# Windowed attention with a soft mixture of experts on one core: loads tied to TensorE's instruction blocks, fewer small matmuls, reordered products

## The chip, the cores and the metric

The kernel runs on one core of a Trainium2 chip. The metric is the device time of one execution in microseconds (us), the median of several runs. TensorE is called PE here, its weight loads PEld, VectorE DVE, ScalarE ACT, GpSimd POOL and SyncE SP. SP issues every transfer of this kernel.

## The reference

Everything is float32. B = 8, H = 8 heads, 512 local and 32 global positions, head dimension 64, and a window of 32 positions to either side.

```python
s_g  = scale * q_g @ concat(k_g, k_l).T           # global queries see all keys
out_g = softmax(s_g) @ concat(v_g, v_l)
s_l  = concat(scale * q_l @ k_g.T, where(|i-j| <= 32, scale * q_l @ k_l.T, -1e9))
out_l = softmax(s_l) @ concat(v_g, v_l)
x = concat(out_g, out_l) as (4352, 512)           # one row per position and batch
logits = x @ phi                                    # 32 slots, 4 per expert
d = softmax over the rows;  c = softmax over the slots
slot_input = d.T @ x                                # 32 x 512
slot_out[e] = relu(slot_input[e] @ w1[e]) @ w2[e]   # 8 experts, 512 -> 1024 -> 512
out = c @ slot_out
```

## The kernel before, in words

The attention works on 32 units, `k` = 0 to 31, each a pair of heads of one batch `b = k // 4` (`s = k % 4` is the unit's place in its batch). The loop over `k` (L428) issues, in the order in which it is written, for each engine:

- loads on SP (L431 to L442): the queries `q` of unit k+1, the keys `k` of unit k+4, the values `v` of one or two later units, once per batch the global queries `qg`, and one or two pairs of expert weight pages `w` (512 KB each; `plan`, L422). Tiles are reused, so a load also waits until the last reader of its buffer is done: `q` has 2 buffers, `k` 5, `v` 4, `qg` 1. SP takes its loads strictly in the order of the program.
- `scores(k)` (L157) on PE: 8 bf16 matmuls write the mask, 32 small matmuls add 32 queries by 128 keys each, into `s`, for which there is one buffer.
- `shift(k)` (L173) on DVE: the row maximum `mx` (L176), then `e = s - mx` in two halves (L179). `e` also has one buffer, and `values(k-1)` reads the previous unit's `e`, so the subtraction waits for that.
- `values(k-1)` (L191) on PE: 32 small matmuls, softmax weights by values (`v` and the two shifted copies `va`, `vb` that POOL makes in `make_v`, L137), one for each 32 queries of a head.
- at s = 0 `global_scores` (L216, 32 matmuls into `gs` and `gm`), then its maximum `gmx` on DVE and its subtraction `sg` on POOL, both halves (L247). At s = 1 `global_transpose`, at s = 2 `global_values` (`og`, L262).
- `normalise(k-1)` (L201) on DVE: two short operations and the product `xh` (L209).
- `transpose_exp(k)` (L182): 8 transposes `t` on PE, two exponentials on ACT.
- `turn_x(k-1)` (L285): 4 transposes `xt` of `xh` on PE, a copy on ACT.
- small work on the logits of the batch before.

A float32 matmul is two weight loads and two matmuls for PE, so four instructions; a transpose or a bf16 matmul is two. The profile's counts of matmuls are after this split.

After the loop come the last logits, the slots' inputs, and the experts: `first_product(0)` (L600, `ph`, experts 0 to 3 side by side), `hidden(0)` (L620, on DVE `hs`, on PE the transposes `ht`, on ACT a copy), `first_product(1)`, `hidden(1)`, then `second_product` (L660, `po`) and the combination of the outputs (`combine`, L681), whose stores go out on SP. The two halves h of the output columns follow each other, and stores of h = 0 run beside matmuls of h = 1.

Of the kernel before, what the change touches and what calls it, by code (L numbers as in the profile page):

```python
# [15 lines left out]
NS = E * SE  # L16
# [25 lines left out]

def window(c):

    w = min(max(c, 1), 14)
    return ((w - 1) % 3, (w - 1) // 3)
# [9 lines left out]
def kernel(  # L56
# [14 lines left out]
    ctx.enter_context(tc.manual_schedule())  # L71

# [30 lines left out]
    npage = [0]  # L103
    slots = [(keep, f"pg{i}") for i in range(NWA // 2)]

    def load_pages():

        pool, tag = slots[npage[0] // 2]
        t = pool.tile([P, 2, 1024], F32, tag=tag, name=f"w{npage[0]}", bufs=1)
        for i in range(2):  # L110
            k, e, a, f = pages[npage[0]]
            nc.sync.dma_start(t[:, i, :], w1[e, a] if k == 0 else w2[e, a, f])
            wt[k, e, a, f] = t[:, i, :]
            npage[0] += 1
# [4 lines left out]
    def load_k(k):  # L119
        ks[k] = kp.tile([P, KC], F32, tag="k", name=f"k{k}", bufs=5)  # L120
        nc.sync.dma_start(ks[k], kT[k])

    def load_q(k):
        qs[k] = kp.tile([P, SL], F32, tag="q", name=f"q{k}", bufs=2)
        nc.sync.dma_start(qs[k], qT[k])

    def load_qg(b):
        qgs[b] = kp.tile([P, P], F32, tag="qg", name=f"qg{b}", bufs=1)
        nc.sync.dma_start(qgs[b], qG[b])
# [27 lines left out]
    def scores(k):  # L157
        ps = psS.tile([P, 2, 4, P], F32, tag="s", name=f"s{k}")
        for i in range(4):
            for r in range(2):  # L160
                nc.tensor.matmul(ps[32 * i:32 * i + 32, r], idm[64 * r:64 * r + 64, :],  # L161
                                 mk[64 * r:64 * r + 64, i:i + 4, :], start=True, stop=False)
        for t in range(4):
            for i in range(4):
                c = 4 * t + i
                for r in range(2):
                    nc.tensor.matmul(ps[32 * i:32 * i + 32, r, t, :], qs[k][64 * r:64 * r + 64, 32 * c:32 * c + 32],  # L167
# [5 lines left out]
    def shift(k):  # L173
# [4 lines left out]
        for r in range(2):  # L178
            nc.vector.tensor_tensor(e[:, r], ps[:, r], bc(mx[:, r], P), ALU.subtract)  # L179
        es[k] = e  # L180

    def transpose_exp(k):  # L182
        for r in range(2):
            pt = psT.tile([P, 4, P], F32, tag="t", name=f"t{k}_{r}")
            for t in range(4):
                nc.tensor.transpose(pt[:, t, :], es[k][:, r, t, :], ident)  # L186
# [4 lines left out]
    def values(k):  # L191
        po[k] = psV.tile([P, 2, 512], F32, tag="v", name=f"o{k}")
        for r in range(2):
            for t in range(4):
                for i in range(4):
                    cls, m = window(4 * t + i)
                    nc.tensor.matmul(po[k][32 * i:32 * i + 32, r, VD * t:VD * t + VD],  # L197
                                     es[k][:, r, t, 32 * i:32 * i + 32], (vs, vas, vbs)[cls][k][:, m, r, :],
                                     start=True, stop=True)
# [16 lines left out]
    def global_scores(b):  # L216
        s = kp.tile([P, 2, 5, P], F32, tag="sg", name=f"sg{b}")
        small = [psT.tile([P, P], F32, tag="t", name=f"gs{b}_{r}") for r in range(2)]
        main = [psT.tile([P, 4, P], F32, tag="t", name=f"gm{b}_{r}") for r in range(2)]

        def mm(dst, j, r, keys):
            nc.tensor.matmul(dst, qgs[b][64 * r:64 * r + 64, 32 * j:32 * j + 32], keys, start=True, stop=True)  # L222

        heads = [(j, r, ks[4 * b + j][64 * r:64 * r + 64, :], slice(32 * j, 32 * j + 32)) for j in range(4) for r in range(2)]
        for j, r, k, o in heads:
            back = bass.AP(k.tensor, k.offset + 32 * 10, [list(k.ap[0]), [-32, 3], [1, 32]])
            mm(small[r][o, 0:96].rearrange("p (a s) -> p a s", s=32), j, r, back)
        for j, r, k, o in heads:
            mm(small[r][o, 96:128], j, r, k[:, 32 * KPOS[14]:32 * KPOS[14] + 32])
        for r in range(2):  # L230
            nc.scalar.copy(s[:, r, 4, :], small[r])
        for a, c0 in ((0, 0), (64, 32 * KPOS[2])):
            for j, r, k, o in heads:
                mm(main[r][o, :, a:a + 64], j, r, k[:, c0:c0 + 256].rearrange("p (m s) -> p m s", s=64))
        for r in range(2):
            nc.scalar.copy(s[:, r, 0:4, :], main[r])  # L236
# [7 lines left out]
    def global_shift(b):  # L244
        for r in range(2):
            s = sg[b][:, r]
            nc.gpsimd.tensor_scalar(s, s, gm[b][:, r:r + 1], None, ALU.subtract)  # L247

    def global_transpose(b):
        pts = psT.tile([P, 2, P], F32, tag="t", name=f"tgs{b}")  # L250
        for r in range(2):
            nc.tensor.transpose(pts[:, r, :], sg[b][:, r, 4, :], ident)
        nc.scalar.activation(sg[b][:, :, 4, :], pts, AF.Exp, scale=SCALE)
        for r in range(2):
            pt = psT.tile([P, 4, P], F32, tag="t", name=f"tg{b}_{r}")
            for m in range(4):
                nc.tensor.transpose(pt[:, m, :], sg[b][:, r, m, :], ident)  # L257
# [4 lines left out]
    def global_values(b):  # L262
        pog[b] = psT.tile([P, 2, VD], F32, tag="t", name=f"og{b}")
        for r in range(2):
            for m in range(5):
                rows = P if m in (0, 4) else 96
                for j in range(4):
                    nc.tensor.matmul(pog[b][32 * j:32 * j + 32, r, :], sg[b][0:rows, r, m, 32 * j:32 * j + 32],  # L268
                                     vs[4 * b + j][0:rows, m if m < 4 else 5, r, :], start=(m == 0), stop=(m == 4))

    def global_normalise(b):
        o = pog[b]
        rc = xp.tile([P, 2], F32, tag="rg", name=f"rg{b}")
        nc.vector.tensor_scalar_add(rc, o[:, :, D], GUARD)
        nc.vector.reciprocal(rc, rc)
        n = xp.tile([P, 2, D], F32, tag="ng", name=f"ng{b}")
        nc.vector.tensor_tensor(n, o[:, :, 0:D], bc(rc, D), ALU.mult)
        p0 = 32 * (b % 4)
        for j in range(4):
            nc.gpsimd.tensor_copy(xg[p0:p0 + 32, P * j:P * j + P].rearrange("p (r d) -> p r d", r=2), n[32 * j:32 * j + 32])  # L280
# [4 lines left out]
    def turn_x(k):  # L285
        pt = psT.tile([P, 4, P], F32, tag="t", name=f"xt{k}")
        for t in range(4):
            nc.tensor.transpose(pt[:, t, :], xhs[k // 2][:, t, P * (k % 2):P * (k % 2) + P], ident)  # L288
# [3 lines left out]
    def turn_xg(i):  # L292
        pt = psT.tile([P, 4, P], F32, tag="t", name=f"xtg{i}")
        for hc in range(4):
            nc.tensor.transpose(pt[:, hc, :], xg[:, P * hc:P * hc + P], ident)
# [3 lines left out]
    def logits_mm(pl, b, hcs):  # L299
        for hc in hcs:  # L300
            for t in range(4):
                nc.tensor.matmul(pl[32 * t:32 * t + 32, :], phisb[:, hc, :], xTs[4 * b + hc][:, t, :],  # L302
                                 start=(hc == 0), stop=(hc == 3))

    def logits_g_mm(pl, i):
        for hc in range(4):
            nc.tensor.matmul(pl[96:128, :], phisb[:, hc, :], xTs["g", i][:, hc, :], start=(hc == 0), stop=(hc == 3))
# [38 lines left out]
    def turn(name, R):  # L346
# [3 lines left out]
        for i in range(2):  # L350
            nc.tensor.transpose(pt[:, i, 0:n], lgs[name][R, i, :], ident[R, R])
# [6 lines left out]
    def slot_sums(b):  # L358
        pa[b] = psT.tile([P, DM], F32, tag="t", name=f"pa{b}")
        for g in range(2):  # L360
            for t in range(4):
                nc.tensor.matmul(pa[b][32 * t:32 * t + 32, 256 * g:256 * g + 256], turned[b][:, 1, 32 * t:32 * t + 32],
                                 xhs[2 * b + g][:, t, :], start=True, stop=True)

    def slot_sums_g(i, p, g):
        nc.tensor.matmul(p[G, 256 * g:256 * g + 256], turned["g", i][:, 1, :], xg[:, 256 * g:256 * g + 256], start=True, stop=True)
# [31 lines left out]
    def turn_combine(b, src, n):  # L398
        pt = psT.tile([P, P], F32, tag="t", name=f"tc{b}")
        nc.tensor.transpose(pt[0:n, :], src, ident)  # L400
# [8 lines left out]
    for _ in range(NWARM):  # L409
        nc.tensor.matmul(pw, wrm[:, 0:P], wrm, start=True, stop=True)  # L410
# [11 lines left out]
    def plan(k):  # L422

        if k < 2:
            return 0
        return 1 if k % 2 == 0 or k > NK - 5 else 0

    for k in range(NK):  # L428
        b, s = k // 4, k % 4
        gb = b if s == 0 else b  # L430
# [360 lines left out]
```

## Time and profile before

| | |
|---|---|
| median of 3 runs | 340.04 us (337.43 to 343.75) |
| the profiled execution | 344.16 us |
| its span, first to last instruction | 342.3 us |
| PE busy (matmuls) | 258.7 us, 76% |
| DVE, POOL, ACT busy | 169.2, 128.6, 105.2 us |
| mean granted clock of PE | 0.915 |

The span is cut by stage in the profile's windows: the units take from 6.3 us to 262 us, the experts and the output the rest. A releaser "issue" after an idle time means that the engine waited for nothing that the profile can show: no semaphore, no other instruction.

### The profile page before, as it was taken

Reading aid. Unit: us, or ns where it says so; the run is one execution under the profiler, and the core shown is the slowest. Engines: PE = TensorE matmul, PEld = TensorE weight load, DVE = VectorE, ACT = ScalarE, POOL = GpSimd, SP = SyncE. Lnnn points to the kernel's source line nnn. Section 1 sums busy time; section 2 is a strip of 40 time slices with the busy share of each in tenths; the row PEclk is TensorE's granted clock in tenths of the full one; section 3 lists DMA queues with packets and bytes.
Section 4 is the critical chain, followed back from the end, with each engine's and each line's share of the span. In section 5 each row is a group of like instructions: output and inputs, shape, how many; then the busy total and the mean of one; then the engine's idle time right before and its main releaser. Section 6 shows DMA issues by size and latency. Waiting matters only on the chain.

```text
span 342.3 us, 15487 instructions
## 1 busy us (share of the span) xinstructions
PE 258.7 (76%) x6984; PEld 188.4 (55%) x6984; DVE 169.2 (49%) x360; ACT 105.2 (31%) x245; POOL 128.6 (38%) x190
## 2 busy tenths in 40 slices
PE   5767788668759779689679767688688897999830
PEld 4556577457637656476467556565676422455620
DVE  1456465645655357567575635467367213115520
ACT  1332244234223333442235213243243202104410
POOL 0375365337434544455385337345543000000000
PEclk9899899969998899999999969999899679999955
DMA  7875695827473647564785629278705959967796
GB/s 252 314 256 146 229 280 187 261 94 265 151 249 129 215 121 251 181 217 142 233 276 188 220 66 312 98 233 269 279 4 192 402 192 405 407 251 264 257 311 214
DMA packets 33761, 77.13 MB, mean 225 GB/s; under 512 B 3232, under 2 KB 13088, under 8 KB 33696
## 3 DMA queue, kind: packets, MB, share of 16 engines
q1 hardware_dynamic: 33696, 76.14, 64.8%
q8 instruction: 55, 0.90, 1.1%
q14 instruction: 10, 0.08, 0.1%
HBM read 67.22 MB, written 8.91 MB: 222 GB/s over the span
## 4 chain that ended last, share of the span: by engine, by line
PE 64%; issue 16%; DVE 10%; DMA 2%; ACT 2%; POOL 1%; SPq 1%; DVEq 0%; ACTq 0%; POOLq 0%
PE o L197 9%; PE s L167 9%; PE t L186 6%; PE xt L288 5%; PE po L665 4%; PE ph L605 4%; PE gm L222 4%; DVE e L179 3%; PE pc L691 3%; PE s L161 3%; PE og L268 3%; PE pl L302 3%; PE tg L257 2%; DMA qg<-in_qG_dram 2%; DVE xh L209 2%
## 5 line engine op out<-in xcount | busy, mean ns | idle before, releaser
L176 DVE TENSOR_REDUCE mx<-s 128x8 f32<-128x1024 f32 x32 | 39.2, 1225 | 60.0 <-PE s L167 59.9
L179 DVE TENSOR_TENSOR e<-s,mx 128x512 f32<-128x512 f32 x64 | 41.2, 686 | 33.8 <-PE o L197 31.5
L141 POOL COPY va<-v 128x650 f32<-128x650 f32 x32 | 23.2, 726 | 91.0 <-issue 52.3
L197 PE MATMUL o<-va,e 128*32 128x65 f32 x768 | 40.3, 227 | 14.9 <-issue 14.9
L187 ACT ACTIVATE e<-t 128x512 f32<-128x512 f32 x64 | 36.2, 603 | 35.3 <-PE t L186 34.1
L197 PE MATMUL o<-vb,e 128*32 128x65 f32 x512 | 38.1, 227 | 8.5 <-issue 8.4
L197 PE MATMUL o<-v,e 128*32 128x65 f32 x768 | 39.7, 227 | 4.9 <-issue 4.9
L167 PE MATMUL s<-k,q 64*32 64x128 f32 x2048 | 39.1, 276 | 3.8 <-issue 3.5
L197 PEld LDWEIGHTS o<-va,e 128*32 128x32 f32 x768 | 32.6, 113 | 13.7 <-issue 13.6
L186 PE MATMUL t<-con,e 128*128 128x128 f32 x256 | 38.3, 289 | 2.1 <-DVE e L179 1.8
L197 PEld LDWEIGHTS o<-v,e 128*32 128x32 f32 x768 | 31.8, 112 | 13.2 <-issue 12.2
L247 POOL TENSOR_SCALAR sg<-sg,gmx 128x640 f32<-128x640 f32 x16 | 29.9, 1883 | 24.0 <-DVE gmx L241 24.0
L167 PEld LDWEIGHTS s<-k,q 64*32 64x32 f32 x2048 | 33.4, 107 | 7.2 <-issue 5.3
L186 PEld LDWEIGHTS t<-con,e 128*128 128x128 f32 x256 | 30.5, 149 | 9.4 <-DVE e L179 5.7
L197 PEld LDWEIGHTS o<-vb,e 128*32 128x32 f32 x512 | 30.1, 112 | 10.1 <-issue 10.1
L288 PE MATMUL xt<-con,xh 128*128 128x128 f32 x128 | 20.3, 279 | 4.8 <-DVE xh L209 3.9
L142 POOL COPY va<-v 32x650 f32<-32x650 f32 x32 | 23.0, 719 | 2.0
L209 DVE TENSOR_TENSOR xh<-o,r 128x512 f32<-128x512 f32 x32 | 22.1, 692 | 1.6
L143 POOL COPY vb<-v 64x520 f32<-64x520 f32 x32 | 19.8, 618 | 1.9
L290 ACT COPY xT<-xt 128x512 f32<-128x512 f32 x32 | 18.9, 592 | 4.8 <-PE xt L288 4.7
L144 POOL COPY vb<-v 64x520 f32<-64x520 f32 x32 | 19.5, 611 | 1.8
L241 DVE TENSOR_REDUCE gmx<-sg 128x2 f32<-128x1280 f32 x8 | 11.9, 1486 | 14.2 <-ACT sg L236 14.2
(160 smaller groups left out, 385.2 us busy)
## 6 DMA issues: line engine op xcount, KB each, us to landing
w<-in_w_dram SPq DMA_DIRECT2D x64, 512.0 KB, 6.8
v<-in_vS_dram SPq DMA_DIRECT2D x32, 390.0 KB, 4.3
k<-in_kT_dram SPq DMA_DIRECT2D x32, 352.0 KB, 4.0
q<-in_qT_dram SPq DMA_DIRECT2D x32, 256.0 KB, 3.6
out_dram<-o SPq DMA_DIRECT2D x16, 512.0 KB, 5.4
qg<-in_qG_dram SPq DMA_DIRECT2D x8, 64.0 KB, 5.1
out_dram<-og SPq DMA_DIRECT2D x16, 32.0 KB, 2.9
con<-in_cst_dram SPq DMA_DIRECT2D x1, 362.0 KB, 4.6
```

What stands on the lines that cost most here:

```text
L141: nc.gpsimd.tensor_copy(va, v[:, 0:5])
L142: nc.gpsimd.tensor_copy(va[0:32], v[0:32, 1:6])
L143: nc.gpsimd.tensor_copy(vb[64:128], v[64:128, 0:4])
L167: nc.tensor.matmul(ps[32 * i:32 * i + 32, r, t, :], qs[k][64 * r:64 * r + 64, 32 * c:32 * c + 32], key_window(k, r, c), start=False, stop= ...
L176: nc.vector.reduce_max(mx, ps, axis=AX.X)
L179: nc.vector.tensor_tensor(e[:, r], ps[:, r], bc(mx[:, r], P), ALU.subtract)
L186: nc.tensor.transpose(pt[:, t, :], es[k][:, r, t, :], ident)
L187: nc.scalar.activation(es[k][:, r], pt, AF.Exp, scale=SCALE)
L197: nc.tensor.matmul(po[k][32 * i:32 * i + 32, r, VD * t:VD * t + VD], es[k][:, r, t, 32 * i:32 * i + 32], (vs, vas, vbs)[cls][k][:, m, r, : ...
L209: nc.vector.tensor_tensor(xhs[u][:, :, P * pp:P * pp + P].rearrange("p t (r d) -> p r t d", r=2), o[:, :, :, 0:D], bc(rc, D), ALU.mult)
L247: nc.gpsimd.tensor_scalar(s, s, gm[b][:, r:r + 1], None, ALU.subtract)
L288: nc.tensor.transpose(pt[:, t, :], xhs[k // 2][:, t, P * (k % 2):P * (k % 2) + P], ident)
```

## The change

1. **Loads in groups.** Every matmul and transpose that the program writes is counted (`counted`), 4 instructions for a float32 matmul and 2 otherwise, from an offset of 63. Where the count passes a multiple of 256, `begin_loads` takes loads from two waiting lists, up to 1,200 KB, and makes each wait for that very matmul. The first list holds `k`, `q`, `v` and `qg`, sorted by the unit that needs them; the second the weight pages, one at a time, which fill what room is left. `begin_due` starts a load without such a wait if no block came in time. `v` gets a fifth buffer, and `q` of unit k+2 is listed as soon as `scores(k)` stands in the program.
2. **Fewer matmuls.** In `values`, the two first and the two last 32-query blocks of a head share their window, so one matmul of 64 queries does both: 28 instead of 32. In `global_scores` one matmul of 512 columns (4 x 2 x 64) takes the place of two of 256: 24 instead of 32.
3. **Subtractions.** `e = s - mx` becomes one DVE instruction of 1,024 elements. Of the global subtraction, one half goes to DVE, the other stays on POOL.
4. **Order.** `turn_x(k-2)` stands between `scores(k)` and `values(k-1)`; before, `turn_x(k-1)` stood at the unit's end. Global work of batch 0 starts at unit 1, and the two halves of `global_values` go to units 2 and 3 of a batch (in the last batch both to unit 2).
5. **First products in a row.** `first_product(1)` follows `first_product(0)` directly; `hidden(0)` comes after it, and `hidden(1)` in the middle of the second product.

```diff
--- before.py
+++ after.py
@@ counting, and starting loads
+OFFSET = 63
+ROOM = 1200
...
+    pe = [OFFSET]
+    lines = [[], []]
+
+    def counted(i, n):
+        pe[0] += n
+        if pe[0] // 256 > (pe[0] - n) // 256:
+            begin_loads(i)
+        return i
+
+    def mm(out, lhsT, rhs, **flags):
+        return counted(nc.tensor.matmul(out, lhsT, rhs, **flags), 2 if lhsT.dtype == BF16 else 4)
+
+    def flip(out, x, idn):
+        return counted(nc.tensor.transpose(out, x, idn), 2)
+
+    def begin_loads(i):
+        room = ROOM
+        lines[0].sort(key=lambda load: load[1])
+        for line in lines:
+            while line and line[0][0] <= room:
+                size, due, load = line.pop(0)
+                room -= size
+                for d in load():
+                    tc.add_manual_dep(d.ins, i.ins.name, mybir.DependencyInfo(
+                        mybir.DependencyClass.Sync, mybir.DependencyReason.DATA))
+
+    def begin_due(k):
+        while any(due <= k for _, due, _ in lines[0]):
+            lines[0].pop(0)[2]()
...
     def load_v(k):
-        vs[k] = vp.tile([P, 6, 2, VD], F32, tag="v", name=f"v{k}", bufs=4)
-        nc.sync.dma_start(vs[k], vS[k])
+        vs[k] = vp.tile([P, 6, 2, VD], F32, tag="v", name=f"v{k}", bufs=5)
+        return [nc.sync.dma_start(vs[k], vS[k])]
@@ shift
-        for r in range(2):
-            nc.vector.tensor_tensor(e[:, r], ps[:, r], bc(mx[:, r], P), ALU.subtract)
+        nc.vector.tensor_tensor(e, ps, bc(mx, P), ALU.subtract)
@@ values
+        for t, i in ((0, 0), (3, 2)):
+            cls, m = window(4 * t + i)
+            for r in range(2):
+                mm(po[k][32 * i:32 * i + 64, r, VD * t:VD * t + VD], es[k][:, r, t, 32 * i:32 * i + 64],
+                   kinds[cls][k][:, m, r, :], start=True, stop=True)
         for r in range(2):
-            for t in range(4):
-                for i in range(4):
-                    cls, m = window(4 * t + i)
-                    nc.tensor.matmul(...)
+            for c in range(2, 14):
+                t, i = c // 4, c % 4
+                cls, m = window(c)
+                mm(...)
@@ global_scores
-        for a, c0 in ((0, 0), (64, 32 * KPOS[2])):
-            for j, r, k, o in heads:
-                mm(main[r][o, :, a:a + 64], j, r, k[:, c0:c0 + 256].rearrange("p (m s) -> p m s", s=64))
+        for j, r, k in heads:
+            four = bass.AP(k.tensor, k.offset, [list(k.ap[0]), [32 * KPOS[2], 2], [64, 4], [1, 64]])
+            product(main[r], j, r, four)
@@ global_shift
-        for r in range(2):
+        for r, eng in ((1, nc.vector), (0, nc.gpsimd)):
             s = sg[b][:, r]
-            nc.gpsimd.tensor_scalar(s, s, gm[b][:, r:r + 1], None, ALU.subtract)
+            eng.tensor_scalar(s, s, gm[b][:, r:r + 1], None, ALU.subtract)
@@ the first loads
+    load_k(1)
+    load_q(1)
     load_v(0)
-    load_k(1)
-    for k in (1, 2, 3):
-        if k > 1:
-            load_k(k)
+    load_k(2)
+    load_k(3)
     load_qg(0)
@@ the loop over k
-        if k + 1 < NK:
-            load_q(k + 1)
-        if k + 4 < NK:
-            load_k(k + 4)
-        for j in {0: (k + 1,), 1: (k + 1, k + 2), 2: (), 3: (k + 1,)}[s]:
-            if j < NK:
-                load_v(j)
-        if s == 1 and b + 1 < B:
-            load_qg(b + 1)
-        for _ in range(plan(k)):
-            if npage[0] < NWA:
-                load_pages()
+        part = global_parts(k)
+        begin_due(k)
         scores(k)
+        line_up("q", k + 2)
+        if k > 1:
+            turn_x(k - 2)
...
         shift(k)
         if k:
             values(k - 1)
-        if s == 0:
+        if "s" in part:
             global_scores(b)
...
-        if s == 2:
-            global_values(b)
+        for r in range(2):
+            if str(r) in part:
+                global_values(b, r)
...
-        if k:
-            turn_x(k - 1)
...
+        line_up_next(k)
+    lines[1].clear()
+    while npage[0] < NWA:
+        load_page()
@@ after the loop
     first_product(0)
+    first_product(1)
...
+    turn_combine(L, turned[L][:, 0, :], P)
+    turn_combine(B, cg.rearrange("p t s -> p (t s)"), 2 * NS)
     hidden(0, 0)
...
-    first_product(1)
-    turn_combine(L, turned[L][:, 0, :], P)
-    turn_combine(B, cg.rearrange("p t s -> p (t s)"), 2 * NS)
-    hidden(1, 0)
...
-    second_product(0, 0, 16)
+    second_product(0, 0, 8)
+    hidden(1, 0)
+    second_product(0, 8, 16)
     slot_outputs(0)
```

On SP, the loads around unit 7 of the kernel before. Names carry the unit (`q8` is the queries of unit 8, `w6` the pair of pages 6 and 7); the words in brackets are the engines and transfers that an instruction waits for.

```order
L125 DMA q8_1158<-in_qT_dram 128x512 [waits DMAHW6_49,PE_49]
L121 DMA k11_1160<-in_kT_dram 128x704 [waits DMAHW7_49]
L133 DMA v8_1162<-in_vS_dram 128x780 [waits DMAHW0_49,PE_49,Pool_49]
L125 DMA q9_1287<-in_qT_dram 128x512 [waits DMAHW2_49,DMAHW1_49,PE_49]
L121 DMA k12_1289<-in_kT_dram 128x704
L133 DMA v9_1291<-in_vS_dram 128x780 [waits DMAHW3_49,Pool_49]
L112 DMA w6_1293<-in_w1_dram 128x1024 [waits DMAHW4_49]
L112 DMA w6_1293<-in_w1_dram 128x1024 [waits DMAHW5_49]
```

The same place in the changed kernel: pages come singly, and each group starts with a load that waits for PE.

```order
L168 DMA q8_1011<-in_qT_dram 128x512 [waits DMAHW3_49,PE_49]
L164 DMA k10_1013<-in_kT_dram 128x704 [waits DMAHW4_49]
L153 DMA w2_893<-in_w1_dram 128x1024 [waits DMAHW5_49]
L164 DMA k11_1123<-in_kT_dram 128x704 [waits DMAHW6_49,PE_49]
L153 DMA w4_1125<-in_w1_dram 128x1024 [waits DMAHW7_49]
L168 DMA q9_1203<-in_qT_dram 128x512 [waits DMAHW0_49,PE_49]
L153 DMA w4_1125<-in_w1_dram 128x1024 [waits DMAHW1_49]
L176 DMA v9_1318<-in_vS_dram 128x780 [waits DMAHW2_49,PE_49,Pool_49]
```

These loads are the groups `q8 k10 w2`, `k11 w4`, `q9 w4` and the start of the one with `v9`; the first load of each waits for PE, and those behind it for no further place in PE's program.

On PE, the end of unit 7 and the start of unit 8 before: the transposes `t7`, then `xt6`, then the masks of `s8`.

```order
L186 MATMUL t7_0_1268<-con_78,e7_1207 128x128 x3
L186 MATMUL t7_1_1274<-con_78,e7_1207 128x128 [waits DVE_49,PE_49]
L186 MATMUL t7_1_1274<-con_78,e7_1207 128x128 x3
L288 MATMUL xt6_1280<-con_78,xh3_1252 128x128 [waits DVE_49,Activation_49]
L288 MATMUL xt6_1280<-con_78,xh3_1252 128x128 x3
L161 LDWEIGHTS con_78
L161 MATMUL s8_1296<-con_78 32x512 [waits PE_49]
L161 LDWEIGHTS con_78
```

The changed kernel, the end of `scores(8)` and the start of `values(7)`. Lines 88 and 91 are the helpers through which every matmul and transpose now goes.

```order
L88 LDWEIGHTS con_78
L88 MATMUL s8_1250<-con_78 32x512
L88 MATMUL s8_1250<-k8_810,q8_1011 32x128 [waits DMAHW6_49,DMAHW3_49]
L88 MATMUL s8_1250<-k8_810,q8_1011 32x128 x31
L91 MATMUL xt6_1291<-con_78,xh3_1213 128x128 [waits DVE_49,Activation_49]
L91 MATMUL xt6_1291<-con_78,xh3_1213 128x128 x3
L88 MATMUL o7_1302<-v7_806,e7_1149 64x65
L88 MATMUL o7_1302<-v7_806,e7_1149 64x65 [waits Activation_49]
```

`xt6` has moved from before `scores(8)` to behind it, and `values(7)` begins with matmuls of 64 queries.

On PE, the experts before: the end of the first product, then the transposes of the hidden layer, then the other first product.

```order
L605 MATMUL ph0_5277<-w12_2248,sT1_5232 32x512 x2
L605 MATMUL ph0_5277<-w14_2562,sT1_5232 32x512 x2
L630 MATMUL ht0_0_5334<-con_78,hs0_5331 128x128 [waits DVE_49]
L630 MATMUL ht0_0_5334<-con_78,hs0_5331 128x128 x3
L630 MATMUL ht0_1_5341<-con_78,hs0_5331 128x128 [waits DVE_49]
L630 MATMUL ht0_1_5341<-con_78,hs0_5331 128x128 x3
L605 MATMUL ph1_5368<-w16_2911,sT0_5231 32x512 x2
L605 MATMUL ph1_5368<-w18_3226,sT0_5231 32x512 x2
```

In the changed kernel the two first products touch.

```order
L88 MATMUL ph0_5133<-w12_2382,sT1_5088 32x512 x2
L88 MATMUL ph0_5133<-w14_2829,sT1_5088 32x512 x2
L88 MATMUL ph1_5171<-w16_3035,sT0_5087 32x512 x2
L88 MATMUL ph1_5171<-w18_3458,sT0_5087 32x512 x2
L88 MATMUL ph1_5171<-w16_3035,sT0_5087 32x512 x2
```

And the second half's hidden transposes stand inside the second product.

```order
L88 MATMUL po2_5272<-w36_4975,hT0_5227 32x256 x2
L88 MATMUL po2_5272<-w38_5040,hT0_5227 32x256 x2
L91 MATMUL ht1_0_5307<-con_78,hs1_5305 128x128 [waits DVE_49]
L91 MATMUL ht1_0_5307<-con_78,hs1_5305 128x128 x3
L91 MATMUL ht1_1_5314<-con_78,hs1_5305 128x128 [waits DVE_49]
L91 MATMUL ht1_1_5314<-con_78,hs1_5305 128x128 x3
L88 MATMUL po2_5272<-w40_5043,hT0_5227 32x256 [waits DMAHW2_49,Activation_49]
```

`ht0` and `ht1` are no longer directly behind the products whose results they turn.

## Rows read from the trace of the kernel before

**Rows 1.** Waits of PE, longest first: who waited for whom, us in total, times, longest.

```profile
PE o L197 <- issue: 28.2, 13, 4.6
PE og L268 <- issue: 7.1, 6, 1.6
PE xt L288 <- DVE xh L209: 3.9, 8, 0.5
PE s L167 <- issue: 3.5, 3, 1.7
PE tgs L252 <- POOL sg L247: 3.4, 3, 1.5
PE gs L222 <- DMA qg<-in_qG_dram: 3.2, 1, 3.2
```

**Rows 2.** Page, DMA queues: packets, MB, share of 16 engines.

```profile
q8 instruction: 55, 0.90, 1.1%
```

**Rows 3.** Timeline of PE, 25.9 to 31 us: start, us, line, xcount, idle before.

```profile
25.93 1.11 PE L268 MATMUL og<-v,sg 96*32 96x65 f32 x61 [0.83 <-issue]
26.97 1.09 PE L186 MATMUL t<-con,e 128*128 128x128 f32 x8
27.90 0.60 PE L288 MATMUL xt<-con,xh 128*128 128x128 f32 x4
28.43 0.41 PE L161 MATMUL s<-con 64*32 64x512 bf16 x8
28.66 0.90 PE L167 MATMUL s<-k,q 64*32 64x128 f32 x46
30.37 0.59 PE L167 MATMUL s<-k,q 64*32 64x128 f32 x18 [0.81 <-issue]
```

**Rows 4.** Chain of waits, pieces in order of time: start us, us, what.

```profile
66.50 4.56 issue
72.26 1.89 PE gm L222 x32
...
170.47 1.07 PE gm L222 x32
...
250.88 0.75 issue
```

**Rows 5.** Windows: us; PE, PEld, DVE, ACT, POOL busy; PEclk, DMA share, GB/s.

```profile
14.89:262.00 247.11, 190.15 (x6195) 151.43 (x6198) 142.75 (x298) 85.98 (x202) 125.13 (x180) 0.94 0.60 200
63.90:68.80 4.90, 2.60 (x130) 2.04 (x129) 1.97 (x5) 0.59 (x1) 0.40 (x1) 1.00 0.91 315
...
248.60:251.60 3.00, 2.28 (x146) 1.92 (x129) 1.90 (x3) 1.02 (x4) 0.83 (x2) 1.00 0.02 5
```

**Rows 6.** Chain of waits through one undisturbed unit, 130 to 136 us.

```profile
130.06 1.29 DVE e L179 x2
...
131.76 0.70 DVE xh L209
...
133.66 0.34 PE s L161 x8
...
134.95 1.05 PE o L197 x64
```

**Rows 7.** Page, costliest groups: busy us, mean ns, idle before, releaser.

```profile
L179 DVE TENSOR_TENSOR e<-s,mx 128x512 f32<-128x512 f32 x64 | 41.2, 686 | 33.8 <-PE o L197 31.5
...
L247 POOL TENSOR_SCALAR sg<-sg,gmx 128x640 f32<-128x640 f32 x16 | 29.9, 1883 | 24.0 <-DVE gmx L241 24.0
```

**Rows 8.** Timeline of PE, 281 to 296.5 us.

```profile
281.08 1.92 PE L605 MATMUL ph<-w,sT 128*32 128x512 f32 x16
285.54 1.32 PE L630 MATMUL ht<-con,hs 128*128 128x128 f32 x8 [2.53 <-DVE hs L627]
286.79 7.07 PE L605 MATMUL ph<-w,sT 128*32 128x512 f32 x64
...
296.04 0.64 PE L665 MATMUL po<-w,hT 128*32 128x256 f32 x8
```

More of the change, by code (lines that the diff above doesn't have):

```diff
@@ L103, with load_page @@
     npage = [0]
+    pair = [None]
     slots = [(keep, f"pg{i}") for i in range(NWA // 2)]
-    def load_pages():
[L108 to L114, printed above, removed]
+    def load_page():
+        n = npage[0]
+        pool, tag = slots[n // 2]
+        if n % 2 == 0:
+            pair[0] = pool.tile([P, 2, 1024], F32, tag=tag, name=f"w{n}", bufs=1)
+        k, e, a, f = pages[n]
+        wt[k, e, a, f] = pair[0][:, n % 2, :]
+        npage[0] += 1
+        return [nc.sync.dma_start(wt[k, e, a, f], w1[e, a] if k == 0 else w2[e, a, f])]
+    def load_pages():
+        for _ in range(2):
+            load_page()
     ks, qs, vs, qgs = {}, {}, {}, {}
@@ L306, in logits_g_mm @@
         for hc in range(4):
-            nc.tensor.matmul(pl[96:128, :], phisb[:, hc, :], xTs["g", i][:, hc, :], start=(hc == 0), stop=(hc == 3))
+            mm(pl[96:128, :], phisb[:, hc, :], xTs["g", i][:, hc, :], start=(hc == 0), stop=(hc == 3))
     G = slice(96, 128)
@@ L409 @@
     for _ in range(NWARM):
-        nc.tensor.matmul(pw, wrm[:, 0:P], wrm, start=True, stop=True)
+        mm(pw, wrm[:, 0:P], wrm, start=True, stop=True)
     load_k(0)
@@ L469 @@
         make_v(k)
-        if s == 0:
+        if "s" in part:
             global_max(b)
             global_shift(b)
-        if s == 2:
-            global_normalise(b)
+        for r in range(2):
+            if str(r) in part:
+                global_normalise(b, r)
         if k == 16:
@@ L488 @@
             combine_sum(("g", 0), cg[:, 0:1, :])
-        if s == 1:
+        if "t" in part:
             global_transpose(b)
@@ L572 @@
     mb = psT.tile([P, 1], F32, tag="t", name="mb")
-    nc.tensor.matmul(mb, mrow4.rearrange("p t s -> p (t s)"), con[0:1, C_ONE:C_ONE + 1], start=True, stop=True)
+    mm(mb, mrow4.rearrange("p t s -> p (t s)"), con[0:1, C_ONE:C_ONE + 1], start=True, stop=True)
     nc.vector.tensor_copy(rt, mb)
@@ L590 @@
         for hc in range(2):
[L591 removed]
+            mm(pst[:, hc, :], acc[:, 256 * i + P * hc:256 * i + P * hc + P], wm, start=True, stop=True)
         (nc.vector.tensor_copy if i else nc.scalar.copy)(sT[i], pst)
@@ L609, in first_product @@
                 tot = psT.tile([P, 1], F32, tag="t", name="tot")
-                nc.tensor.matmul(tot, qmat, wl, start=True, stop=True)
+                mm(tot, qmat, wl, start=True, stop=True)
                 nc.vector.tensor_scalar_add(rt, tot, GUARD)
@@ L673, in slot_outputs @@
         pq = psT.tile([P, 256], F32, tag="t", name=f"pq{h}")
-        nc.tensor.matmul(pq, qmat, so, start=True, stop=True)
+        mm(pq, qmat, so, start=True, stop=True)
         sas[h] = fin.tile([P, 256], F32, tag=f"sa{h}", name=f"sa{h}")
```

142 lines of the change are left out of this document (84 added, 58 removed).

## The prediction

> **What bounds the kernel now.** I read PE's waits first, then the DMA queues, then PE's timeline to see what the unexplained waits have in common, then the windows beside them, then the chain of waits.
>
> PE's longest waits have no releaser [rows 1]: 28.2 us in 13 waits in the values, 7.1 in 6 in the global values, 3.5 in 3 in the scores. Together that is 38.8 us in 22 waits; smaller groups I leave out. A queue of its own moved 0.90 MB in 55 packets, 16.4 KB each, marked as instructions [rows 2]. The timeline between two such waits, at 25.93 and 30.37 us, holds 61 + 8 + 4 + 8 + 46 = 127 matmuls, each with its weight load, so 254 instructions [rows 3], and 16.4 KB for some 256 instructions would be 64 bytes each. So PE seems to run out of program at the end of each block of 256, and the waits are those for the next block's transfer.
>
> How long PE waits hangs on the other transfers. The longest wait of all, 4.56 us [rows 4], follows a stretch in which the DMA engines were 0.91 busy; a wait of 0.75 us [rows 4] ends a stretch with a share of 0.02 [rows 5]. I take 0.75 us as what a dense block costs with free queues, and the rest as the time in which 16 KB stand behind megabytes.
>
> [...]
>
> **The change part by part.** All durations are of the profiled execution, 344.16 us (span 342.3 and 1.9 around it); that is 4.1 us over the median of the runs, 340.04.
>
> 1. Loads in groups. A group starts behind the matmul that opens a block, so the fetch of the next block, asked for at that time, should stand ahead of it. The 22 waits keep 0.75 us each, 16.5, and lose 38.8 - 16.5 = 22.3 us. Ends: nothing (the loads meet the fetches anyway) and all 38.8 (the rest hides in other waits). I take **-22.3**, since the quiet stretch shows that remainder directly.
>
> 2. Fewer matmuls. The 64 of one unit's values take 1.05 us [rows 6]; four products less are 8 of these 64, 0.13 us, and 32 units make 4.2 us. The global scores lose 8 of 32 products a batch, but their columns stay, so I give them nothing. Instructions fall by 8 x 2 x 32 for the values and 16 x 2 x 8 for the global scores, 768 or three blocks, at 0.75 each 2.3 us. **-6.5**; ends 0 (a wait for DVE fills the space) and -9.5 (three blocks at the present mean of 38.8/22 = 1.76 us, plus 4.2).
>
> 3. The move of the `xt` transposes and the single subtraction. In an undisturbed unit DVE's subtraction ends at 130.06 + 1.29 = 131.35 us, and PE begins the next unit's masks at 133.66 [rows 6], 2.31 us later, because `xt` first waits for `xh`, which ends at 132.46. In the new order the masks follow the 8 transposes, 27.90 - 26.97 = 0.93 us [rows 3]; with a hand-over about 1.0, so 1.3 us less. Against it: `xt` takes 28.43 - 27.90 = 0.53 us [rows 3] ahead of the values, for which the subtraction waits (31.5 us of DVE's idle time there [rows 7]); and the transposes lose their early start on the first half, half of 0.93. Net 1.3 - 0.53 - 0.47 = 0.3 us a unit, 31 units: **-9**. Ends: +6 (0.2 worse a unit, where the global work hides the gain) and -25 (0.8 better, where the values don't wait for `xt` but run under DVE's maximum).
>
> 4. The clock. [...] The global scores took 1.89 us directly after the longest wait and 1.07 us elsewhere [rows 4], so long waits are followed by slow work. [...]
>
> 5. The global subtraction. POOL loses 8 of its 16 instructions of 1.88 us [rows 7], and PE's 3.4 us of waiting for them [rows 1] can go. DVE gets 8 of 128x640; not in the trace, by its 686 ns for 512 elements [rows 7] 0.86 us each, 6.9 in all, delaying the next unit's maximum at most by that. DVE is busy 142.75 of 247.11 us there, so part is covered. **0**; ends -3.4 and +6.9.
>
> 6. The start. Batch 0's global scores move to unit 1, so the wait of 3.2 us for `qg` [rows 1] is gone: **-3.2**; ends -3.2 and 0, if `v0`, now behind three more loads, holds POOL instead.
>
> 7. The experts. Between the first products PE stands or transposes from 283.00 to 286.79 us, and from 293.86 to 296.04 before the second one [rows 8], 5.97 us together. Afterwards 1.3 us for each half's transposes and 0.4 for two others remain, 3.0: **-2.9**, the subtractions and copies running beside the products. The code from the second product to the stores is the same, so the end comes that much earlier; ends 0 and -3.4.
>
> 8. What grouping costs. The largest groups hold 1,170 KB, 1.20 MB. At 315 GB/s for a share of 0.91 [rows 5], 346 GB/s when full, that takes 3.5 us. The blocks of the units average (247 - 47) / 46 = 4.3 us, so a group usually ends in its block; where a dense block is over sooner, the next fetch still meets its tail. The wait is on SP: a load behind a group's first waits for PE too, and through it `scores` of a later unit. Queries are listed more than a unit ahead, and a group moves in 3.5 us, less than a unit. I take **+3**; ends 0 and +20, about 0.4 us in each block.
>
> Sum: -22.3 - 6.5 - 9 - 6 + 0 - 3.2 - 2.9 + 3 = -46.9, so 297.3 us in an execution like the profiled one, and 4.1 less for the median: **293 us**.
>
> **Rivals.**
>
> *The unit's chain takes it back.* When PE no longer waits for program, it waits for DVE: one buffer for the scores and one for `e` tie the units to maximum, values, subtraction, transposes. For it: the subtraction already waits 31.5 us for the values. Against it: DVE is busy 58% of the stage. Half of terms 1 and 4 and none of 2 and 3: -11 - 3 - 3.2 - 2.9 + 3 = -17, so 323 - 4 = about 319 us.
>
> *The rest hides too.* The blocks' last 0.75 us fall where PE waits for the subtraction anyway. Then term 1 is -38.8, 16.5 more: 277 us.
>
> *The count goes astray.* An instruction that waits twice may take a place in the program of its own; 101 of the changed kernel's PE instructions wait for two things, and the count leaves them out. At the end of the units groups would start some 90 instructions, a third of a block, late. If half of term 1's gain is lost for it, 11 us: 304 us.
>
> [...]
>
> *Loads come too late.* This one is slower. A load now starts only where PE has reached a place, and SP is in order, so one late group delays all behind it; if `q`, `k` or `v` land after they are wanted, PE stands, and reaches the next place later still. A whole group late is 3.5 us; half the units so, 16 x 3.5 = 56 us, gives 349 us. It decides from 47/3.5, some 13 units, on. Against it: only one transfer, the first `qg`, now holds PE for more than 3 us, and the mean DMA share of the stage is 0.60 [rows 5].
>
> **How the numbers follow.** The forecast has 0.48, the chain 0.17, the hidden rest 0.15, the count 0.10, other waits 0.05, late loads 0.05. The likeliest alone spans 284 to 304 us. With the chain and the rest's hiding within it the range is 276 to 319 us, which leaves about 0.15 outside. A measurement of this kernel tells about 2% from no change, so faster means under 333 us: nearly all cases but late loads, less the chance that several terms come out at their poor ends, 0.92. Within 2% is 0.04, slower 0.04.
>
> **What would show it.** Right: PE's waits without releaser fall from 38.8 us in these three groups to about 16, none much over 1.5 us; the granted clock of the units goes above 0.94; `xt` no longer waits for `xh`; the first products touch. Wrong: waits without releaser stay above 30 us (term 1); PE's waits for the subtraction or for POOL grow by more than 15 us (the chain); PE waits for `q`, `k` or `v` transfers (late loads); waits without releaser grow towards the end of the units (the count).

## The result and the profile after

The changed kernel takes 295.2 us, the median of four runs (292.14 to 300.01), beside 340.76 us for the kernel before: a ratio of 0.8661, 95% interval 0.8532 to 0.879. The forecast was 293 us. The profiled execution is the longest of the four, 300.01 us, at the lowest granted clock (0.947; the others 0.958 to 0.970), as that of before, 344.16, stood above its median; the two traces are compared with each other. A second trace of the changed kernel, of 296.22 us, belongs to the second measurement further on, and is named where it says something else.

The page of the changed kernel: span, busy time of each engine, the queue of the program's blocks, the engines' shares of the chain that ended last, and two groups of instructions (busy us, mean ns, idle before, releaser).

```profile
span 297.8 us, 14686 instructions
...
PE 255.7 (86%) x6600; PEld 181.9 (61%) x6600; DVE 174.5 (59%) x360; ACT 106.2 (36%) x245; POOL 121.6 (41%) x214
...
q8 instruction: 52, 0.85, 1.1%
...
PE 81%; issue 6%; DVE 4%; ACT 2%; DMA 1%; POOL 1%; SPq 0%; DVEq 0%; POOLq 0%; ACTq 0%
...
L221 DVE TENSOR_TENSOR e<-s,mx 128x1024 f32<-128x1024 f32 x32 | 39.2, 1224 | 25.2 <-PE o L88 21.5
...
L296 POOL TENSOR_SCALAR sg<-sg,gmx 128x640 f32<-128x640 f32 x8 | 17.3, 2164 | 12.0 <-DVE gmx L290 12.0
```

The span fell by 44.5 us and PE's busy time by 3.0 (from 258.7), so 41.5 us of the gain are time in which PE had stood. Three blocks fewer went through the queue of instructions [rows 2].

Waits of PE in the changed kernel: who waited for whom, us in total, times, longest.

```profile
PE o L88 <- issue: 5.4, 6, 2.3
PE t L91 <- DVE e L221: 5.2, 6, 2.7
PE og L88 <- issue: 3.2, 4, 1.2
PE s L88 <- issue: 2.8, 4, 1.3
PE pl L88 <- issue: 2.3, 2, 1.4
...
PE tgs L91 <- POOL sg L296: 0.8, 1, 0.8
```

The three groups of [rows 1] went from 38.8 us to 5.4 + 3.2 + 2.8 = 11.4. All waits without a releaser, the small groups too, went from 46.9 us in 28 to 15.1 in 18. The waits for `xh` (3.9) and for `qg` (3.2) are gone, that for POOL is 0.8 instead of 3.4; the transposes' wait for the subtraction grew from 1.8 to 5.2. In the kernel before it was this:

```profile
PE t L186 <- DVE e L179: 1.8, 4, 1.1
```

What PE's waits without a releaser are for stands in the traces themselves, in the times of the single packets of `q8`. In the kernel before, each of the 28 waits ends 1.2 to 1.6 us after such a packet has landed, and in the changed kernel each of the 18 ends 1.3 to 1.6 us after one. The packet takes about 1.0 us in both (median). What differs is its start: the packet after the end of such a wait starts 1.05 to 6.7 us later before, and 1.05 to 2.9 us later in the changed kernel. So PE does wait for its program, and the transfer of the program is late because it starts late.

Windows, units 1 to 30 before, then of the changed kernel unit 0, units 1 to 30, the last unit to the first product, and the rest. Columns as in [rows 5].

```profile
14.89:254.35 239.46, 183.39 (x5967) 146.42 (x5966) 137.80 (x288) 82.60 (x196) 121.10 (x172) 0.94 0.61 202
```

```profile
6.10:13.04 6.94, 4.24 (x81) 3.29 (x81) 2.45 (x2) 1.86 (x2) 2.68 (x4) 1.00 0.71 225
13.04:211.38 198.34, 181.26 (x5659) 139.67 (x5658) 142.93 (x286) 84.96 (x199) 113.33 (x192) 0.99 0.74 236
211.38:232.20 20.82, 17.09 (x301) 11.82 (x300) 9.85 (x29) 6.84 (x20) 4.75 (x12) 0.84 0.87 327
232.20:297.80 65.60, 49.10 (x545) 24.55 (x544) 18.96 (x43) 12.53 (x26) 0.64 (x2) 0.84 0.86 314
```

The same cuts before, by the first masks of units 0, 1 and 31 and the first product, are 8.60, 239.46, 19.29 and 68.66 us. So units 0 to 30 gave 42.8 us (8.0 to 6.6 us each), the end 3.1, and the stretch between them took 1.5 more (19.35 us in the second trace, as before). In the units PE is granted 0.99 of its clock instead of 0.94 and is busy 0.91 of the time instead of 0.77.

The chain of waits of the changed kernel (start us, us, what): the values of one clean unit, then the longest remaining wait.

```profile
91.47 1.21 PE o L88 x56
...
96.98 0.59 PE xt L91 x4
97.56 0.97 PE o L88 x38
98.54 2.33 issue
100.87 0.47 PE o L88 x17
```

The transposes `xt` now run straight into the values. The 2.33 us wait lies in a stretch that the windows show thus:

```profile
98.30:100.90 2.60, 0.27 (x21) 0.10 (x11) 0.00 (x0) 0.00 (x0) 0.00 (x0) 1.00 0.98 367
```

The DMA engines are 0.98 busy there. The load of `q15` had come due, and `v16` stood ahead of it in the list, so both were started without the wait for a block, at 93.90 and 93.43 us, behind groups of 1,036 and 1,158 KB. They landed at 101.06 and 99.80, and the program's packet started only at 98.61.

Timeline of PE in the changed kernel, the experts:

```profile
232.21 7.04 PE L88 MATMUL ph<-w,sT 128*32 128x512 f32 x48
239.19 0.38 PE L88 MATMUL tot<-wl,con 128*128 128x1 f32 x2
239.50 8.79 PE L88 MATMUL ph<-w,sT 128*32 128x512 f32 x80
```

The first products touch; the 2.53 us in front of `ht` [rows 8] are not there.

### The profile page after: what moved, and what is told of

Same layout as the page of the kernel before. It is cut to its first block, busy times and chain, and to the rows that moved or that the text cites. A ratio compares the mean times of both kernels' runs of the same rounds, so it can differ in the third digit from the quotient of the medians.

```text
span 297.8 us, 14686 instructions
## 1 busy us (share of the span) xinstructions
PE 255.7 (86%) x6600; PEld 181.9 (61%) x6600; DVE 174.5 (59%) x360; ACT 106.2 (36%) x245; POOL 121.6 (41%) x214
## 4 chain that ended last, share of the span: by engine, by line
PE 81%; issue 6%; DVE 4%; ACT 2%; DMA 1%; POOL 1%; SPq 0%; DVEq 0%; POOLq 0%; ACTq 0%
PE s L88 15%; PE o L88 14%; PE t L91 11%; PE xt L91 6%; PE ph L88 5%; PE po L88 5%; PE pc L88 4%; DVE e L221 3%; PE pl L88 3%; PE og L88 3%; PE pa L88 3%; PE gm L88 3%; PE tg L91 2%; DMA con<-in_cst_dram 1%; PE gs L88 1%
## 5 line engine op out<-in xcount | busy, mean ns | idle before, releaser
L221 DVE TENSOR_TENSOR e<-s,mx 128x1024 f32<-128x1024 f32 x32 | 39.2, 1224 | 25.2 <-PE o L88 21.5
L88 PE MATMUL o<-va,e 128*32 128x65 f32 (+1 forms) x640 | 41.9, 228 | 4.0 <-issue 4.0
L88 PE MATMUL o<-v,e 128*32 128x65 f32 (+1 forms) x640 | 43.7, 227 | 0.5 <-issue 0.5
L91 PE MATMUL t<-con,e 128*128 128x128 f32 x256 | 37.1, 287 | 5.5 <-DVE e L221 5.2
L88 PEld LDWEIGHTS o<-v,e 128*32 128x32 f32 (+1 forms) x640 | 34.2, 116 | 6.5 <-issue 6.2
L88 PEld LDWEIGHTS o<-va,e 128*32 128x32 f32 (+1 forms) x640 | 33.6, 117 | 6.8 <-issue 4.5
L88 PE MATMUL o<-vb,e 128*32 128x65 f32 x512 | 29.7, 224 | 0.9 <-issue 0.9
L88 PEld LDWEIGHTS o<-vb,e 128*32 128x32 f32 x512 | 23.5, 111 | 1.1 <-issue 1.1
L296 POOL TENSOR_SCALAR sg<-sg,gmx 128x640 f32<-128x640 f32 x8 | 17.3, 2164 | 12.0 <-DVE gmx L290 12.0
L328 POOL COPY xg<-ng 32x64 f32<-32x64 f32 x64 | 15.0, 234 | 6.5 <-DVE ng L325 3.5
```

The costliest lines, as they stand in the source:

```text
L88: return counted(nc.tensor.matmul(out, lhsT, rhs, **flags), 2 if lhsT.dtype == BF16 else 4)
L91: return counted(nc.tensor.transpose(out, x, idn), 2)
L221: nc.vector.tensor_tensor(e, ps, bc(mx, P), ALU.subtract)
L296: eng.tensor_scalar(s, s, gm[b][:, r:r + 1], None, ALU.subtract)
```

## The experiments

Unless another figure is given, "waits for program" are all of PE's waits without a releaser: 46.9 us before, 15.1 after (12.7 in the second trace). The first measurement of `xt` at the unit's end, of the old matmuls, of the first products apart and of the two subtractions had no changed kernel beside it, and the kernel before took 334.9 to 346.0 us in it. Differences of a few us in these times show little, and the traces are read by stage instead.

**Loads without the wait.** The same loads, issued at the same places of the program, but not held back by the matmul.

```diff
-                for d in load():
-                    tc.add_manual_dep(d.ins, i.ins.name, ...)
+                load()
```

> The changed kernel with its loads in the same order on SP, but none of them waits for a matmul that opens a block; each starts as soon as its buffer is free. Fetch theory (the 16 KB of program stand behind loads): PE's waits without releaser go back to 35 us or more from about 15, and the time rises by 18 to 30 us, to 313 to 325 us. Rival, the waits are no fetches: within 2% of 295 us. Rival, the loads' new order alone does it: also within 2% of 295 us, with waits near 15 us.

Measured: 309.49 us, ratio 0.900 (0.8931 to 0.907) to 344.35 before; waits for program 24.8 us in 21. The direction is that of the fetch theory, the size is less: about 14 us hang on the wait itself (the changed kernel with an exact count took 295.31 us on the same chip). Waits of 35 us or more and 313 us or more had been forecast.

**Half a block off.** Each load waits for a matmul in the middle of a block; the size and spacing of the groups stay.

```diff
-OFFSET = 63
+OFFSET = 63 + 128
```

> The changed kernel with an offset of 191 instead of 63, so each group starts behind a matmul in the middle of a block, 128 instructions late. Fetch theory: a group then still runs when the next block begins, so the fetches are late by some 0.3 to 0.6 us in most of 46 blocks, 305 to 320 us, and waits without releaser rise to 22 to 35 us. Rival, spacing (what helps is that loads come in limited groups, wherever they start): within 2% of 295 us.

Measured: 317.41 us, ratio 0.9238 (0.9155 to 0.932); waits for program 30.2 us in 30. PE's longest waits in it:

```profile
PE s L88 <- issue: 10.1, 11, 2.1
PE o L88 <- issue: 9.2, 8, 2.4
```

That is 22 us more than the changed kernel from the phase alone, and worse than no wait at all. The packets of `q8` are as long as before (median 1.0 us), but behind a wait they start 1.45 to 4.2 us after PE goes on, with a median of 2.7 instead of 1.4. Spreading the loads is not what helps; where in a block they start is.

**An exact count.** 104 of PE's instructions get an instruction ahead of them that only waits, and it takes a place in the program: counted with these (135 of them in the kernel before), the 28 waits for program before and the 18 after all stand 192 or 193 instructions behind a multiple of 256; counted without them, at 73 to 183. Here they are counted too.

```diff
-OFFSET = 63
+OFFSET = 65
+WAITS = {26, 74, 106, 158, ...}
...
     def counted(i, n):
+        n += calls[0] in WAITS
+        calls[0] += 1
         pe[0] += n
```

> The changed kernel with a count that includes the instructions which only wait (104 in all, and two before the first matmul), so that groups start at the blocks' real beginnings up to the end. Rival, the count goes astray: 5 to 11 us faster than the changed kernel, 284 to 290 us, above all in units 16 to 31. Forecast: within 1% (292 to 298 us), since a group 90 instructions late still ends before most fetches.

Measured: 295.31 us, ratio 0.8555 (0.8453 to 0.8657). A second measurement stood beside the changed kernel:

> The exact count again. Rival, the count goes astray: 5 us or more under the changed kernel in the same call. Forecast: within 3 us of it.

It gave 294.82 us, 0.8408 (0.8314 to 0.8502). The count makes no difference that can be seen.

**The groups alone.** Parts 2 to 5 of the change are undone; the grouped loads, the fifth buffer of `v` and the early listing of `q` stay, and so do the first loads' new order and the global values' work by single heads (24 instructions more on DVE, 32 more on POOL than before).

```diff
-        nc.vector.tensor_tensor(e, ps, bc(mx, P), ALU.subtract)
+        for r in range(2):
+            nc.vector.tensor_tensor(e[:, r], ps[:, r], bc(mx[:, r], P), ALU.subtract)
...
-            for c in range(2, 14):
+            for c in range(16):
...
-        for r, eng in ((1, nc.vector), (0, nc.gpsimd)):
+        for r, eng in ((0, nc.gpsimd), (1, nc.gpsimd)):
...
-        if k > 1:
-            turn_x(k - 2)
```

> The kernel before with the loads in groups alone (and the fifth buffer for v and the global values of the two heads apart, which that needs): matmuls as many as before, xt at the unit's end, the subtractions as before, global work at the units as before, the first products apart. Forecast by terms 1, 4 and 8: 340.8 - 22.3 - 6 + 3 = 315.5 us (307 to 322). Rival, the unit's chain takes it back: 325 us or more, with PE's waits for DVE's subtraction and for xh grown by 10 us or more.

Measured: 323.12 us, ratio 0.941 (0.9338 to 0.9481), 21 us less than before. PE's waits:

```profile
PE o L88 <- issue: 17.2, 14, 2.2
PE og L88 <- issue: 7.1, 6, 2.3
...
PE tgs L91 <- POOL sg L293: 5.4, 5, 1.6
PE xt L91 <- DVE xh L253: 4.1, 8, 0.5
...
PE s L88 <- issue: 3.2, 5, 1.0
```

The three groups keep 17.2 + 7.1 + 3.2 = 27.5 us, not 16.5. The time misses the forecast of 307 to 322 us, and the rival does not hold either: the waits for `xh` (4.1) and for the subtraction (2.1) are about what they were. Some 4 us are lost at the start, where global work of batch 0 still stands in unit 0 and PE waits 5.7 us for `qg`. PE is busy 249.0 us instead of 258.7 with the same matmuls; 5.5 of these 9.7 us are in units 1 to 30 (177.9 instead of 183.4), where the granted clock is 0.98 instead of 0.94, the rest mostly behind the units.

**`xt` at the unit's end again.** The rest of the change stays.

```diff
-        if k > 1:
-            turn_x(k - 2)
...
+        if k:
+            turn_x(k - 1)
```

> The changed kernel with the xt transposes back at the unit's end (of unit k-1, behind the transposes of unit k). Forecast, term 3 without the merged subtraction: 9 us slower, all of it in PE's waits for xh and in the gap between subtraction and next masks, waits without releaser unchanged near 15 us. Rival, hiding (the slow transposes between scores and values gave the next block time to arrive): 12 to 20 us slower, and waits without releaser rise by 8 us or more.

Measured: 305.12 us, before 343.0. Waits for program 20.1 us in 20; the wait for `xh` does not come back, five short ones for ACT take its place:

```profile
PE o L88 <- issue: 11.2, 9, 3.5
...
PE xt L91 <- ACT e L229: 1.3, 5, 0.3
```

Units 0 to 30 take 213.1 us instead of 205.2, and 203.4 in the second trace. So the place of `xt` is worth 8 to 10 us, about half of them in blocks that arrive late.

**The old matmuls.** Values and global scores as before.

```diff
-        for t, i in ((0, 0), (3, 2)):
-            ...
-            for c in range(2, 14):
+            for c in range(16):
...
-        for j, r, k in heads:
-            four = ...
+        for a in range(2):
+            for j, r, k in heads:
+                four = ...
```

> The changed kernel with 32 products in the values and 32 in the global scores, as before. Forecast, term 2: 6.5 us slower (4.2 in the values' own time, 2.3 for three more blocks). Rival, PE's space is filled by waiting for the subtraction: within 2 us.

Measured: 302.11 us, before 343.0. The four runs lie between 296.7 and 306.01 us and overlap with those of the changed kernel, so the time alone does not place it; in the profiled execution, the longest of the four, units 0 to 30 take 215.0 us instead of 205.2 (203.4 in the second trace). Page, waits and chain of this kernel:

```profile
PE 250.4 (82%) x6984; PEld 181.3 (60%) x6984; DVE 174.8 (57%) x360; ACT 106.4 (35%) x245; POOL 121.3 (40%) x214
```

```profile
PE og L88 <- issue: 8.1, 6, 2.0
PE o L88 <- issue: 6.8, 8, 1.7
...
PE s L88 <- issue: 5.0, 8, 1.4
```

```profile
109.33 1.05 PE o L88 x64
```

This is the run that I learned most from. With more matmuls PE is busy 250.4 us, *no more* than with the fewer (250.4 to 255.7 in four traces of the changed kernel, with and without the exact count), and yet its units take longer: its waits for program are 25.7 us, 10.6 more. The chain tells why: 64 matmuls of 32 queries take 1.05 us, the 56 of the changed kernel 1.21, and all values together keep PE busy for 39.4 us here and for 43.9 there. Fewer matmuls are slower here, and by the units' time it pays. That it pays because the slower values leave each block more time is an argument from these numbers; the run also undoes the global scores.

**The first products apart.** The order of part 5 undone.

```diff
     first_product(0)
-    first_product(1)
...
+    first_product(1)
+    hidden(1, 0)
```

> The changed kernel with the order of the experts as before (hidden layer directly behind each first product). Forecast, term 7: 2.9 us slower, all after the first product's start, units unchanged.

Measured: 300.5 us, ratio 0.8896 (0.8717 to 0.9075). The timeline of PE:

```profile
232.67 5.36 PE L88 MATMUL ph<-w,sT 128*32 128x512 f32 x48
...
242.72 1.31 PE L91 MATMUL ht<-con,hs 128*128 128x128 f32 x8 [2.53 <-DVE hs L703]
243.97 7.07 PE L88 MATMUL ph<-w,sT 128*32 128x512 f32 x64
```

The wait of 2.53 us is back. From the first product to the end it takes 299.5 - 232.67 = 66.8 us, 1.2 more than the changed kernel, although its first 48 matmuls ran in 5.36 instead of 7.04 us; without these 1.7 us it would be 2.9. With the two products in a row this stretch takes 63.3 to 65.6 us in ten traces (the smaller groups further on left out); in the other order it takes 66.8 here, 66.6 in the groups alone and 68.7 before. The interval is too wide to say more from the time.

**Two subtractions.** `e = s - mx` in halves again.

```diff
-        nc.vector.tensor_tensor(e, ps, bc(mx, P), ALU.subtract)
+        for r in range(2):
+            nc.vector.tensor_tensor(e[:, r], ps[:, r], bc(mx[:, r], P), ALU.subtract)
```

> The changed kernel with the subtraction in two halves again, so that the first four transposes start under the second half. By term 3 the early start is worth 0.47 us a unit where the chain goes through the subtraction, up to 14 us faster in 31 units; if PE is held by its own work and by blocks instead, within 3 us of the changed kernel, and PE's waits for the subtraction (5.2 us) fall by 2 to 5 us either way.

Measured: 301.56 us, ratio 0.8931 (0.877 to 0.9093), too wide to place, so it was measured again beside the changed kernel.

> The subtraction in two halves again. Hiding theory (the wait for the whole subtraction gives blocks time to arrive, so merging costs nothing): slower than the changed kernel by 2 to 6 us, waits without releaser higher by 3 us or more. Rival, the merged subtraction costs 0.47 us a unit: up to 14 us faster.

> The changed kernel again, on the chip of the three that follow, as their measure. 0.853 to 0.879 of the kernel before, as at first; PE's waits without releaser 13 to 20 us in all.

Two halves: 297.52 us, 0.8687 (0.8637 to 0.8738). The changed kernel: 293.9 us, 0.8535 (0.8455 to 0.8615). PE's waits in the two, the halves first:

```profile
PE o L88 <- issue: 6.8, 8, 1.4
PE og L88 <- issue: 3.2, 4, 1.5
PE s L88 <- issue: 3.2, 5, 0.9
...
PE t L91 <- DVE e L222: 2.1, 1, 2.1
```

```profile
PE t L91 <- DVE e L221: 5.2, 6, 2.7
PE o L88 <- issue: 4.9, 5, 1.7
PE s L88 <- issue: 2.8, 4, 1.6
PE og L88 <- issue: 2.3, 4, 1.1
```

With halves PE waits 3.1 us less for DVE, and in all 16.7 instead of 12.7 us for program. What the early start gains is lost again in waits for blocks. The kernel is 3.6 us slower by the medians, and all six runs with halves (from 296.33 us) lie above all six without (up to 296.22). The two traces, whose spans are 0.6 us apart, do not show where the rest of the 3.6 us lies.

**Smaller groups.** Exact count, and 1,000 instead of 1,200 KB for a group. Fewer weight pages find room in the units; those left over load after the last unit.

```diff
-ROOM = 1200
+ROOM = 1000
```

> The exact count and groups of at most 1,000 KB instead of 1,200, so 14 of the 34 early weight pages are loaded after the last unit. Fetch theory: smaller groups are over sooner, 2.9 instead of 3.4 us, so fewer blocks are late: units 3 to 8 us faster in all, and the pages still come before the first products need them, so 3 to 8 us faster than the exact count. Rival: the pages left over hold the first products, PE waits for transfers of w by 5 us or more, and the time is the same or slower.

Measured: 295.3 us, ratio 0.8608 (0.8552 to 0.8663). Waits for program fall to 7.0 us in 7, and units 0 to 30 take 192.0 us, where the changed kernel, measured beside it, takes 203.4. The end gives it back. Its waits of PE, its chain, and its window from the first product on:

```profile
PE po L92 <- DMA w<-in_w_dram: 4.3, 9, 0.7
PE og L92 <- issue: 3.8, 3, 2.4
```

```profile
203.69 8.75 DMA w<-in_w_dram
...
222.81 10.08 DMA w<-in_w_dram
...
253.32 10.19 DMA w<-in_w_dram
```

```profile
217.20:263.60 46.40, 41.10 (x430) 16.85 (x430) 10.73 (x29) 6.33 (x14) 0.64 (x2) 0.96 1.03 409
```

From 203.7 to 263.5 us the chain is nothing but pages, one transfer behind the other at 409 GB/s. The first product starts at 217.27 us instead of 229.04, and from there to the end it takes 74.8 instead of 65.1.

## Why the prediction was right

The sum was 297.3 us for an execution like the profiled one; it took 300.01. For the median it was 293; it came to 295.2, and 293.9 in the second measurement. Inside the sum three steps were wrong, in terms 1, 2 and 3, and they made up for each other: the mechanism was right, and that the sum came within 3 us is in part luck.

**Term 1, loads in groups (-22.3).** The mechanism holds: behind a wait the next block's packet starts 1.05 to 2.9 us after PE goes on, and with the phase shifted by half a block the same loads cost 22 us more. The size was that of the whole change, not of this part. The step "the 22 waits keep 0.75 us each, 16.5" failed for the groups alone, which keep 27.5. The rest went when the other parts gave the blocks time. The 0.75 us of a quiet stretch is no fixed price: by `q8` the next packet needs at least 1.05 us to start after PE goes on, about 1.0 to land, and PE goes on 1.2 to 1.6 us behind it, some 3.5 us together (an estimate). By it a block whose work takes longer need not wait at all, and the changed kernel has waits of only 0.2 us. The groups alone save 21 us with the clock, everything but the wait saves 35 (344.35 to 309.49), the two together 46 to 52; the parts overlap by 4 to 10 us, so no term belongs to one part alone.

**Term 2, fewer matmuls (-6.5).** Undoing it makes units 0 to 30 10 to 12 us longer in the traces and the median 7 us longer, too uncertain to be held against 6.5; what it does is done in another way. The step "four products less are 8 of these 64, 0.13 us" has the wrong sign: the values went from 1.05 to 1.21 us, 32 x 0.16 = 5.1 us more. What seems to pay is that 112 instructions in 1.21 us use up a block more slowly than 128 in 1.05, and that there are fewer of them: the waits are 10.6 us less. The global scores did stay at 1.07 us, as assumed.

**Term 3, `xt` and the single subtraction (-9).** Both of its steps were mis-sized, and the errors offset each other. The move alone stood in it with 1.3 - 0.53 = 0.77 us a unit, some 24 us in 31 units, and measured 8 to 10. The 0.47 us a unit charged for the lost early start, some 15 us, was wrong: what an early start gains goes into waits for blocks, and the halves are 3.6 us slower.

**Term 4, the clock (-6).** No run shows these 6 us; what the runs show is this. The granted clock of the units rose from 0.94 to 0.99. Where the matmuls are the same as before, units 1 to 30 keep PE busy for 177.9 us (groups alone) and 179.0 (old matmuls) instead of 183.4. So 4.4 to 5.5 us came back where the term had 6; another 4 came back outside them, which it did not count. In the changed kernel the slower values hide most of it: 181.3 us, and 180.8 in the second trace.

**Terms 5 to 7.** The global subtraction (0): DVE's share took 0.55 us, not the 0.86 estimated, and PE's wait for POOL fell by 2.6; no run takes it by itself. The start (-3.2): from unit 0's first masks to unit 2's it takes 13.8 instead of 16.1 us, 2.3 less. The experts (-2.9): 3.1 less. Not priced was that one `turn_x` now stands behind the loop, ahead of the last unit's values; the stretch from the last unit to the first product is 1.5 us longer in the first trace and as long as before in the second, so no cost can be seen.

**Term 8, grouping's cost (+3).** The 2.33 us wait behind 0.98 busy DMA engines is of its kind. The smaller groups had 7.0 us of waits left, so at least 5 of the changed kernel's 12.7 to 15.1 hang on the size of groups or the pages among them; the run changed both. The 46 blocks of this term are those of the changed kernel; the kernel before runs some 48 in that window, 4.1 us each.

**The rivals.** The chain did not take the gain back: the waits for the subtraction grew by 3.4 us, not 15. Its price was added up wrongly, 4.1 us being taken off twice: 344.16 - 17.1 - 4.1 is 323 us, not 319, and the range should have ended there; the result is far from either. The rest did not hide, 11.4 us of the three groups remain. The count was tried and makes no difference. That the waits were something other than fetches falls with the half block, which cost 22 us, and with the packets of `q8`, 1.2 to 1.6 us behind which every one of them ends. No load of `q`, `k` or `v` holds PE in the changed kernel, so none came too late.

No experiment beat the changed kernel by more than its measurement's uncertainty. Still open is a version with small groups whose pages are all there before the end; it was not tried.

## What to carry to other kernels

When an engine waits and the trace shows no releaser, count the instructions between such waits: if it is the same number, or a multiple of it, the program itself may be late, and its transfer may compete with your loads (here the 46 such waits of the two kernels stood 192 or 193 instructions behind a multiple of 256, and the one of 2.33 us fell where the DMA engines were 0.98 busy). The times of the packets that carry instructions decide it: here every such wait of either kernel ended 1.2 to 1.6 us behind one. Try to start large loads just behind the fetch: here the same loads half a block off cost 22 us. Where such waits bound a stretch, ask whether a faster engine only waits longer: here values of 1.05 us in 64 matmuls went with 25.7 us of waits, values of 1.21 us in 56 with 15.1, and the fewer and slower ones seem to have paid. A part of such a change measured alone can tell little about its share in the whole: here the groups alone saved 21 us, everything but the wait 35, the two together 46 to 52.

## What was not expected

A matmul of 64 queries by 65 columns is not cheaper than two of 32: 56 matmuls in 1.21 us, 64 in 1.05, in nearly every undisturbed unit of the kernels that have them.

The global subtraction, split between two engines, in the changed kernel (durations in ns: shortest, median, longest; first and last start):

```profile
L296 DVE TENSOR_SCALAR sg<-sg,gmx x8: 552/553/553, 21.5 to 199.6; 128x640 f32<-128x640 f32 x8
L296 POOL TENSOR_SCALAR sg<-sg,gmx x8: 2157/2165/2168, 21.7 to 199.8; 128x640 f32<-128x640 f32 x8
```

DVE needs a quarter of POOL's time for the same tile, and POOL needs 0.28 us more than before [rows 7], in each of the eight, with DVE at work beside it. The groups alone, where POOL does both halves, have a median of 1,882 ns, so the 0.28 us come with the split and not with the loads; no run here shows what causes them.
